# MLP 1's first pair: the second batch by Strassen's scheme, with the orders of VectorE and ScalarE written out

## The chip, the cores and the metric

The kernel runs on one core of one Trainium2 chip. The metric is the device time of one execution in microseconds (us), the median of several runs. The engines are called as in the profile: PE is TensorE (PEld its weight loads), DVE is VectorE, ACT is ScalarE, POOL is GpSimd, SP is SyncE, whose queue issues the DMAs here.

## What the kernel must compute

Clustered attention on 2 batches of 8 heads, whose output `x` (1536 tokens of 512) goes through two MLPs. The change is in the first one and at its seam to the second:

```python
x = np.ascontiguousarray(attn_out.transpose(0, 2, 1, 3)).reshape(B * S, H * D)
h = x @ w_in                            # MLP 1: 1536 x 512 by 512 x 2048
g = h * (1.0 / (1.0 + np.exp(-h)))
x = g @ w_out                           # 2048 x 512
gate = 1.0 / (1.0 + np.exp(-(x @ w_gate)))   # MLP 2, hidden width 1536
out = (gate * (x @ w_val)) @ w_out2
```

## The kernel before

**Precision.** Every fp32 operand is split into a rounded part `hi` and a rest `lo` (fp32r). A product is then three chains of matmuls, hi·hi, hi·lo and lo·hi. ACT makes `hi` by a cast (L65), DVE or POOL makes `lo` by a subtraction (L81 for x and its sums, L1003 for the silu's result, L807 for weights).

**Products.** MLP 1 works in 8 pairs of blocks of 128 hidden units. `x` is stored transposed, as four quarters "11", "12", "21", "22" (half of the model width by half of a batch's tokens); a quarter of one batch is 128 x 768, its halves of a token range 384 wide. `strassen` computes the 2 x 2 block product with 7 products, called x, y, z, w, X, v, W in the order of issue, instead of 8: each has 6 matmuls of 128 x 384 for each batch. Products y, z, w and v take sums of weights (`wi0s`, `wi0t`, ...) and sums of x's quarters (`T1` to `T4`; split into `t1` to `t4`). Their results are put together by additions on DVE (L957), a copy by ACT (L967, of product x) and silu on ACT (L1026). A name such as `h_0y` is product y of the call that begins at batch 0; the trace uses it for both batches when one call does both (128 x 768). The tensors `gha` and `gla` are the hi and lo of silu's result, and `wi2s` is the hi (ACT) and lo (POOL) of the weight sum s for pair 2.

**The first pair** is mixed with the end of the attention. Batch 0 goes through Strassen's scheme there, beside the last attention heads. Batch 1 is finished by the last attention products, and is computed by `direct` (tiles `p`, L1013): the plain 2 x 2 block product, two groups of 24 matmuls. `T1` to `T4` of batch 1 are made later (L94 to L105), since pair 1 is the first to need them. After that come the output products y (L1064) of the first pair, per batch, and from then on each pair's first two h products (`steps(following, n=2)`: x and y), then the output products of the pair before (`mixed`), then the other five.

**Weights** arrive by DMA as 64-bit words (`ri`, `ro`, two buffers) and are converted in integer passes: ACT casts (L764), POOL clamps (L767), DVE makes three passes (L778, L780, L782; for the gate L775 and L782), then ACT and POOL split the result, and POOL makes the sums `si` (L827 to L830).

**Order.** In the first pair and all of MLP 1, `tc.manual_schedule` fixes PE's order to that of the code; the other engines' orders come from the scheduler. Lists such as `behind` and `paced` put an instruction of a conversion behind a given other instruction in that order (`behind` those of DVE, `paced` those of ACT), one entry for one instruction. Every engine executes its own row of instructions strictly in that order.

Of the kernel before, what the change touches and what calls it, by code (L numbers as in the profile page):

```python
# [32 lines left out]
def clustered_attention_then_two_mlps(ctx, tc, qT, kT, v, cen, cenT, w1i, w1o, w2g, w2v, w2o, out):  # L33
# [55 lines left out]
    def right_sums(temporary, name, b, caster, adder, kept):  # L89

        put = partial(right_operand, name, b, caster=caster, subber=adder)
        b11, b21, b12, b22 = quarters(b).values()
        t1 = temporary(f"{name}t1{b}")
        adder.tensor_tensor(t1, b12, b11, op=ALU.subtract)  # L94
        kept[b] = t1
        t2 = temporary(f"{name}t2{b}")
        adder.tensor_tensor(t2, b22, t1, op=ALU.subtract)
        put("t2", t2)
        yield
        t4 = temporary(f"{name}t4{b}")  # L100
        adder.tensor_tensor(t4, t2, b21, op=ALU.subtract)
        put("t4", t4)
        yield
        t3 = temporary(f"{name}t3{b}")
        adder.tensor_tensor(t3, b22, b12, op=ALU.subtract)  # L105
        put("t3", t3)
        yield

    def scheme_operands(temporary, name, b, caster, adder):
# [26 lines left out]
        return make  # L136

    def right_last(name, b, src, caster, subber):
        right_operand(name, b, "t1", src, caster, subber)

    rp = ctx.enter_context(tc.tile_pool(name="rp", bufs=2))
    with ExitStack() as att:
# [861 lines left out]

    def direct(w, name, take, b):

        for m in range(2):
            o = bank(f"{name}_{b}{m}", (ppa, ppb)[m])
            for h in range(2):
                for r in range(2):  # L1010
                    for k in range(KQ):
                        for n, (s, t) in enumerate(((0, 0), (0, 1), (1, 0))):
                            nc.tensor.matmul(  # L1013
                                o[:, h, 0:HS],
                                lhsT=w[f"a{m + 1}{r + 1}"][s][:, k, :],
                                rhs=right[b, f"{r + 1}{h + 1}"][t][:, k, :],
                                start=r == 0 and k == 0 and n == 0,
                                stop=r == 1 and k == KQ - 1 and n == 2,
                            )
            take(o[:, :, 0:HS], m, b)  # L1020
            yield
# [9 lines left out]
    def hidden_directly(i, b):  # L1031
        def take(c, m, b):
            g = temporary(f"g{i}_{m}_{b}")
            nc.scalar.activation(g, c, AF.Silu)
            split(g, m, (slice(0, 2), b), f"a{i}", nc.vector)

        yield from direct(weights("1i", i), f"p{i}", take, b)

# [35 lines left out]
    def gated(i, bs, together=False):  # L1074
# [7 lines left out]
        def value(c, m, h, bs, inside):  # L1082
# [135 lines left out]
    def sums(name, b):
        return right_sums(temporary, name, b, ACT, DVE, kept)

    def last(name, b):
        right_last(name, b, kept.pop(b), ACT, DVE)

# [52 lines left out]

    subs = []

    def rounding(m, h):
        late.pop((m, h))(subs)  # L1280

    def splitting():
        subs.pop(0)()

    def split_now(m, h):
        late.pop((m, h))()
# [135 lines left out]
```

## Time and profile before

| | us |
|---|---|
| median of 3 runs | 768.45 (768.21 to 768.61) |
| the profiled execution: own time / span | 767.51 / 765.7 |
| PE busy / weight loads | 755.2 (99%) / 648.9 (85%) |
| DVE busy | 597.7 (78%) |
| ACT busy | 425.9 (56%) |
| POOL busy | 389.7 (51%) |
| granted clock of PE | full in all 40 slices |

Busy time is the sum over an engine's instructions, and the profiled execution's own time holds 1.8 us outside the span. The shares are means over stages with different limits; the stages that the change touches lie between 230 and 320 us (end of the attention, pairs 0 to 2) and about 445 us (last pair of MLP 1 before MLP 2's gate begins).

### The profile page before, as it was taken

Reading aid. Unit: us, or ns where it says so; the run is one execution under the profiler, and the core shown is the slowest. Engines: PE = TensorE matmul, PEld = TensorE weight load, DVE = VectorE, ACT = ScalarE, POOL = GpSimd, SP = SyncE. Lnnn points to the kernel's source line nnn. Section 1 sums busy time; section 2 is a strip of 40 time slices with the busy share of each in tenths; the row PEclk is TensorE's granted clock in tenths of the full one; section 3 lists DMA queues with packets and bytes.
Section 4 is the critical chain, followed back from the end, with each engine's and each line's share of the span. In section 5 each row is a group of like instructions: output and inputs, shape, how many; then the busy total and the mean of one; then the engine's idle time right before and its main releaser. Section 6 shows DMA issues by size and latency. Waiting matters only on the chain.

```text
span 765.7 us, 11470 instructions
## 1 busy us (share of the span) xinstructions
PE 755.2 (99%) x4289; PEld 648.9 (85%) x4290; DVE 597.7 (78%) x773; ACT 425.9 (56%) x742; POOL 389.7 (51%) x361
## 2 busy tenths in 40 slices
PE   8999999999999999999999999999999999999997
PEld 4766776677767998998989989999999989999896
DVE  7887887788788968798978587986697767859566
ACT  6777776776886762534615545565544525353320
POOL 5235134644655773566647456125776745565430
PEclk9999999999999999999999999999999999999999
DMA  7677457447122122132222120010313112111104
GB/s 209 168 210 192 115 151 195 117 128 193 45 77 72 66 83 83 41 125 83 83 83 73 66 82 1 29 56 27 110 56 108 58 55 97 68 57 56 55 1 166
DMA packets 25488, 71.61 MB, mean 94 GB/s; under 512 B 4484, under 2 KB 4952, under 8 KB 25432
## 3 DMA queue, kind: packets, MB, share of 16 engines
q1 hardware_dynamic: 24888, 70.84, 30.7%
q8 instruction: 34, 0.56, 0.3%
q14 instruction: 22, 0.18, 0.1%
q10 hardware_dynamic: 544, 0.03, 0.0%
HBM read 48.01 MB, written 3.19 MB: 67 GB/s over the span
## 4 chain that ended last, share of the span: by engine, by line
PE 92%; DVE 3%; ACT 2%; DMA 1%; issue 1%; POOL 0%; SPq 0%; ACTq 0%
PE z L1134 13%; PE s L501 8%; PE v L551 7%; PE t L538 5%; PE y L1064 4%; PE h_0w L943 4%; PE h_0x L943 4%; PE v_0x L943 3%; PE g_0w L943 3%; PE g_0x L943 3%; PE v_0w L943 3%; PE y_00None L1064 2%; PE y_21None L1064 2%; PE y_20None L1064 2%; PE y_11None L1064 2%; PE y_10None L1064 2%
## 5 line engine op out<-in xcount | busy, mean ns | idle before, releaser
L514 ACT ACTIVATE e<-s,nm 128x768 f32<-128x768 f32 x96 | 86.5, 901 | 33.8 <-DVE nm L509 32.7
L509 DVE TENSOR_REDUCE nm<-s 128x1 f32<-128x768 f32 x96 | 91.4, 953 | 10.3 <-PE s L501 8.6
L1134 PE MATMUL z<-wu,ghb 128*128 128x512 f32 (+1 forms) x292 | 89.1, 387 | 0.0
L551 PE MATMUL v<-ph,vv 128*64 128x384 f32 x384 | 69.0, 495 | 0.1
L1134 PEld LDWEIGHTS z<-wu,ghb 128*128 128x128 f32 x292 | 54.5, 188 | 10.8
L501 PE MATMUL s<-ka,qa 128*128 128x384 f32 x192 | 57.5, 380 | 2.0 <-ACT e L514 1.5
L538 PE MATMUL t<-ident,e 128*128 128x128 f32 x384 | 58.4, 275 | 0.1
L1134 PE MATMUL z<-wu,glb 128*128 128x512 f32 (+1 forms) x146 | 56.7, 388 | 0.0
L538 PEld LDWEIGHTS t<-ident,e 128*128 128x128 f32 x384 | 44.9, 140 | 11.3 <-issue 9.0
L551 PEld LDWEIGHTS v<-ph,vv 128*64 128x64 f32 x384 | 24.7, 136 | 32.7 <-issue 29.0
L501 PE MATMUL s<-k,q 128*128 128x384 f32 x192 | 49.6, 339 | 0.0
L65 ACT ACTIVATE ph<-t 128x512 f32<-128x512 f32 x68 | 40.6, 598 | 12.6 <-PE t L538 12.0
L1043 DVE TENSOR_TENSOR acc<-z,acc 128x1024 f32<-128x1024 f32 x24 | 29.2, 1221 | 21.6 <-PE z L1134 21.6
L68 DVE COPY ph<-u 128x512 f32<-128x512 f32 x48 | 32.7, 682 | 16.3 <-PE u L528 16.3
L582 POOL TENSOR_TENSOR acc<-xf,rb 128x768 f32<-128x768 f32 x7 | 12.9, 1837 | 59.2 <-DMA rb<-d_rb 56.5
L807 POOL TENSOR_TENSOR wu<-cu,wu 128x512 fp32r<-128x512 f32 x12 | 16.3, 1356 | 52.0 <-ACT wu L65 52.0
L807 POOL TENSOR_TENSOR wo<-co,wo 128x512 fp32r<-128x512 f32 x16 | 24.1, 1510 | 33.5 <-ACT wo L65 33.4
L501 PEld LDWEIGHTS s<-k,q 128*128 128x128 f32 x192 | 34.5, 188 | 0.5 <-DMA k<-rows 0.3
L501 PEld LDWEIGHTS s<-ka,qa 128*128 128x128 f32 x192 | 28.9, 190 | 6.9 <-ACT e L514 5.9
L1064 PE MATMUL y<-gha,wo 128*128 128x384 f32 x128 | 32.8, 334 | 0.0
L1134 PEld LDWEIGHTS z<-wu,glb 128*128 128x128 f32 x146 | 27.4, 188 | 6.0 <-DVE glb L1003 0.5
L563 DVE TENSOR_TENSOR xf<-v,other 64x384 f32<-64x384 f32 x32 | 17.7, 553 | 14.8 <-ACT other L560 14.3
(709 smaller groups left out, 2151.9 us busy)
## 6 DMA issues: line engine op xcount, KB each, us to landing
ri<-in_w1i SPq DMA_DIRECT2D x16, 512.0 KB, 3.2
ro<-in_w1o SPq DMA_DIRECT2D x16, 512.0 KB, 3.1
ka<-kh SPq DMA_DIRECT2D x32, 192.0 KB, 3.6
rg<-in_w2g SPq DMA_DIRECT2D x12, 512.0 KB, 3.6
rv<-in_w2v SPq DMA_DIRECT2D x12, 512.0 KB, 3.1
ru<-in_w2o SPq DMA_DIRECT2D x12, 512.0 KB, 3.2
qq<-in_qT SPq DMA_DIRECT2D x8, 384.0 KB, 3.6
kk<-in_kT SPq DMA_DIRECT2D x8, 384.0 KB, 4.1
```

Source lines behind the costliest of these rows:

```text
L65: return nc.scalar.activation(o, i, AF.Copy)
L68: return nc.vector.tensor_copy(o, i)
L501: nc.tensor.matmul(s[:, g, 0:HS], lhsT=a[:, j, i * P : (i + 1) * P], rhs=c[:, j, g * HS : (g + 1) * HS], start=n == 0, stop=n == 1,)
L509: maxima.append(nc.vector.tensor_reduce(nm, s[:, :, 0:HS], axis=AX.XY, op=ALU.max, negate=True))
L514: x = nc.scalar.activation(e, s[:, :, 0:HS], AF.Exp, bias=nm, scale=1.0, accum_out=tots[p][:, n : n + 1])
L538: nc.tensor.transpose(t[:, kt, :], e[:, kt * P : (kt + 1) * P], ident)
L551: m = nc.tensor.matmul(o[(L, U)[kt % 2]], lhsT=vv[:, j, kt, :], rhs=ring[:, kt, g * G : (g + 1) * G], start=n < 2, stop=n >= NT - 2,)
L807: nc.gpsimd.tensor_tensor(lo, src, hi, op=ALU.subtract)
L943: nc.tensor.matmul(o[:, b, 0:HS], lhsT=w[a][s][:, k, :], rhs=right[b, q][t][:, k, :], start=start and k == 0 and n == 0, stop=k == KQ - 1 ...
L1043: added.append(nc.vector.tensor_tensor(z if to is None else to, o, z, op=ALU.add))
L1064: nc.tensor.matmul(o[:, d, 0:width], lhsT=s[:, d, k, :], rhs=t[:, c], start=k == 0 and m == 0, stop=k == 1 and m == 2,)
L1134: nc.tensor.matmul(o[:, a, c], lhsT=s[:, q * P : (q + 1) * P], rhs=r[:, c], start=k == 0 and m == 0, stop=k == 1 and m == 2, skip_group_ch ...
```

## The change

Batch 1 of the first pair goes through `strassen` too, in the order x, X, y, z, w, v, W, with its products set between those of batch 0. Its operands `T1` to `T4`, `t1` to `t4`, 21 and 22 are made before that, in an order that the code now writes out for DVE and ACT as well, up to the last `lo` of the first pair. Quarter "12" of batch 1 is no longer split by itself (it serves only as `t1`). The DVE passes of pair 1's `ci` weights stand behind the last `lo` of the first pair (`behind.extend(parted * 6)`). The passes of the gate's first weights (`cg`) stand behind a later DVE addition, that of h_7's d of the first batch (`sum_of_w`). The line numbers move: L957 becomes L939, L967 L949, L81 L114, L1003 L985 (L1202 in the first pair), L1026 L990, L1064 L1024, L764 L743, L778/780/782 L757/759/761, L563/637 L540/615.

```diff
-    def direct(w, name, take, b):
-        for m in range(2):
-            o = bank(f"{name}_{b}{m}", (ppa, ppb)[m])
...
-    def hidden(i, bs, order="xyzwXvW"):
+    def hidden(i, bs, order="xyzwXvW", apart=False):
         def take(c, m, h, bs, inside):
             g = c if inside else temporary(f"g{i}_{m}{h}{bs.start}")[:, bs]
             nc.scalar.activation(g, c, AF.Silu)
-            split(g, m, (h, bs), f"a{i}", nc.gpsimd if m and h else nc.vector)
+            parts = partial(split, g, m, (h, bs), f"a{i}", nc.gpsimd if m and h else nc.vector)
+            if apart:
+                late[bs.start, m, h] = parts
+            else:
+                parts()
...
+                if c == place["2g", 0]:
+                    behind.extend(sum_of_w * 4)
...
-    for q in ("11", "12"):
-        right_quarter("x", 1, q, POOL, POOL)
-    for q in ("21", "22"):
-        right_quarter("x", 1, q, ACT, DVE)
-    front = hidden(0, ONE[0], "xwXyzvW")
-    steps(front, n=1)
+    right_quarter("x", 1, "11", POOL, POOL)
+    one = scheme_operands(temporary, "x", 1, ACT, DVE)
+    with tc.issue_after(finished[0].ins):
+        one("T1")
+    zeroth = partial(steps, hidden(0, ONE[0], "xwXyzvW", True))
+    zeroth(n=1)
     look[0] = AHEAD
     weights("1i", 0)
-    steps(front, n=5)
-    following = hidden_directly(0, 1)
-    next(following)
-    run(front)
-    run(following)
+    order = tc.manual_schedule(engines={mybir.EngineType.PE, mybir.EngineType.DVE, mybir.EngineType.Activation})
+    first = partial(steps, hidden(0, ONE[1], "xXyzwvW", True))
+    one("+21")
+    zeroth(n=1)
+    one("+22")
+    zeroth(n=1)
+    one("T2", "T3", "+t2")
+    zeroth(n=1)
+    one("t2", "+t3")
+    rounding(0, 0, 0)
+    zeroth(n=1)
+    first(n=1)
+    one("+t1")
+    splitting(0, 1, 1)
+    one("21", "t3")
+    zeroth(n=1)
+    rounding(0, 1, 0)
+    one("T4", "+t4", "t1")
+    zeroth(n=1)
+    first(n=1)
+    rounding(0, 0, 1)
+    paced.extend(rounded * 2)
+    first(n=1)
+    one("t4", "22")
+    splitting(0, 0, 0)
+    splitting(0, 1, 0)
+    rounding(1, 0, 0)
+    first(n=2)
...
+    order = tc.manual_schedule(engines={mybir.EngineType.PE})
+    order.__enter__()
+    behind.extend(parted * 6)
     weights("1o", 0, 1)
-    rest = sums("x", 1)
-    next(rest)
-    with tc.issue_after(parted[0].ins):
-        run(rest)
-    last("x", 1)
     run(mixed(0, 0))
     run(mixed(0, 1))
     run(hidden(1, ALL))
     for i in range(2, N1):
         following = hidden(i, ALL) if i < N1 - 1 else hidden(i, ONE[0], "xyzXwvW")
         steps(following, n=2 if i < N1 - 1 else 5)
+        if i == N1 - 1:
+            sum_of_w[:] = critical[-1:]
         run(mixed(i - 1, first=int(i == N1 - 1)))
```

How the change moves instructions is shown at three places. The first is DVE from the last attention products (`xf`, and the product into `acc` that completes `x` of batch 1) to the `lo` of the first silu result, `gla_0` from `g_000`. The first output product y needs that `lo` in its second matmul. `x_...` and `xt_...` are `lo` of a quarter or of a sum, `xtt_...` the sums T1 to T4. Before:

```order
L563 TENSOR_TENSOR xf_2780<-v_1_1_2914,other_1_1_2921 64x384
L637 TENSOR_TENSOR acc<-xf_2780,rb_1_2927 128x384
L81 TENSOR_TENSOR x_3047<-acc,x_3047 128x768
L957 TENSOR_TENSOR h_0u_3054<-h_0y,h_0u_3054 128x384
L778 TENSOR_SCALAR ci_0_3208<-ci_0_3208 128x512
L81 TENSOR_TENSOR x_3050<-acc,x_3050 128x768
L957 TENSOR_TENSOR h_0u_3111<-h_0z,h_0u_3054 128x384
L1003 TENSOR_TENSOR gla_0_3100<-g_000_3097,gha_0_3099 128x384
L780 SCALAR_TENSOR_TENSOR ci_0_3208<-ri_0_3206,ci_0_3208 128x512
L778 TENSOR_SCALAR ci_1_3216<-ci_1_3216 128x512
L957 TENSOR_TENSOR h_0d<-h_0w,h_0u_3111 128x384
L782 SCALAR_TENSOR_TENSOR ci_0_3208<-ri_0_3206,ci_0_3208 128x512
```

After, the same place, first half:

```order
L96 TENSOR_TENSOR xtt_3044<-acc 128x768
L540 TENSOR_TENSOR xf_2780<-v_1_1_2914,other_1_1_2921 64x384
L615 TENSOR_TENSOR acc<-xf_2780,rb_1_2927 128x384
L96 TENSOR_TENSOR xtt_3099<-acc,xtt_3044 128x768
L96 TENSOR_TENSOR xtt_3101<-acc 128x768
L939 TENSOR_TENSOR h_0u_3047<-h_0y,h_0u_3047 128x384
L114 TENSOR_TENSOR xt_3103<-xtt_3099,xt_3103 128x768
L939 TENSOR_TENSOR h_0u_3119<-h_0z,h_0u_3047 128x384
L939 TENSOR_TENSOR h_0d<-h_0w,h_0u_3119 128x384
L114 TENSOR_TENSOR x_3080<-acc,x_3080 128x768
```

And directly on, to that `lo`:

```order
L114 TENSOR_TENSOR xt_3114<-xtt_3101,xt_3114 128x768
L939 TENSOR_TENSOR h_0u_3119<-h_0u_3119,h_0v 128x384
L96 TENSOR_TENSOR xtt_3158<-xtt_3099,acc 128x768
L114 TENSOR_TENSOR xt_3140<-xtt_3044,xt_3140 128x768
L939 TENSOR_TENSOR h_0u_3047<-h_0w,h_0u_3047 128x384
L939 TENSOR_TENSOR h_1u_3132<-h_1y,h_1u_3132 128x384
L114 TENSOR_TENSOR xt_3160<-xtt_3158,xt_3160 128x768
L114 TENSOR_TENSOR x_3089<-acc,x_3089 128x768
L1202 TENSOR_TENSOR gla_0_3117<-g_000_3097,gha_0_3116 128x384
```

Ahead of `gla_0` from `g_000` there now stand four sums T and six `lo` of batch 1, each 128 x 768, where there stood two `lo`; the passes of `ci` are gone from between. On PE, the output product y that takes this `lo` stands right behind the first matmul of product v of batch 1 (tile `h_1v`).

The second place is ACT around the rounding of pair 2's weight sums, `wi2s` and `wi2t`. `h_0u_3564` (after: `h_0u_3578`) is the copy of pair 2's product x, the silu on `h_0u_3394` (after: `h_0u_3408`) that of pair 1's last product W; PE issues pair 2's x, then pair 2's y, which takes `wi2s`. Before:

```order
L65 ACTIVATE wi2s<-si_3527 128x512
L764 ACTIVATE co_1_3554<-ro_1_3552 128x512
L65 ACTIVATE gha_0_3471<-g_000_3469 128x768
L65 ACTIVATE wi2t<-si_3527 128x512
L1026 ACTIVATE h_0u_3422<-h_0u_3422 128x768
L65 ACTIVATE gha_1_3453<-h_0u_3422 128x768
L1026 ACTIVATE h_0u_3394<-h_0u_3394 128x768
L967 ACTIVATE h_0u_3564<-h_0x 128x768
L65 ACTIVATE gha_0_3471<-h_0u_3394 128x768
```

After:

```order
L990 ACTIVATE h_0u_3436<-h_0u_3436 128x768
L743 ACTIVATE co_0_3557<-ro_0_3555 128x512
L65 ACTIVATE gha_1_3467<-h_0u_3436 128x768
L990 ACTIVATE h_0u_3408<-h_0u_3408 128x768
L949 ACTIVATE h_0u_3578<-h_0x 128x768
L743 ACTIVATE co_1_3568<-ro_1_3566 128x512
L65 ACTIVATE gha_0_3485<-h_0u_3408 128x768
L65 ACTIVATE wi2s<-si_3541 128x512
L65 ACTIVATE wi2t<-si_3541 128x512
```

The rounding of `wi2s` stood seven rows ahead of the copy of pair 2's x, and stands three rows behind it now. On DVE, the six passes of pair 2's `ci` weights, of which `wi2s` is made, now stand together between pair 1's additions d and v; the `lo` of two silu results and the addition of product W follow.

The third place is DVE at the last pair of MLP 1, with the passes of `cg`, the gate's first weights; the addition that makes `h_0u_4834` (after: `h_0u_4848`) from `h_0y` frees the bank of the output product `y_00None` that opens the next `mixed`. Before:

```order
L775 SCALAR_TENSOR_TENSOR cg_0_5062<-cg_0_5062,rg_0_5060 128x512
L782 SCALAR_TENSOR_TENSOR cg_0_5062<-rg_0_5060,cg_0_5062 128x512
L957 TENSOR_TENSOR h_0d<-h_0w,h_0u_4692 128x768
L957 TENSOR_TENSOR h_0u_4692<-h_0u_4692,h_0v 128x768
L1003 TENSOR_TENSOR gla_0_4742<-g_000_4739,gha_0_4741 128x768
L957 TENSOR_TENSOR h_0u_4580<-h_0w,h_0u_4580 128x768
L775 SCALAR_TENSOR_TENSOR cg_1_5070<-cg_1_5070,rg_1_5068 128x512
L782 SCALAR_TENSOR_TENSOR cg_1_5070<-rg_1_5068,cg_1_5070 128x512
L1003 TENSOR_TENSOR gla_1_4724<-h_0u_4692,gha_1_4723 128x768
L957 TENSOR_TENSOR h_0u_4834<-h_0y,h_0u_4834 128x384
L957 TENSOR_TENSOR h_0u_4850<-h_0z,h_0u_4834 128x384
L1003 TENSOR_TENSOR gla_0_4742<-h_0u_4580,gha_0_4741 128x768
```

After:

```order
L939 TENSOR_TENSOR h_0u_4706<-h_0u_4706,h_0v 128x768
L985 TENSOR_TENSOR gla_0_4756<-g_000_4753,gha_0_4755 128x768
L939 TENSOR_TENSOR h_0u_4594<-h_0w,h_0u_4594 128x768
L985 TENSOR_TENSOR gla_1_4738<-h_0u_4706,gha_1_4737 128x768
L939 TENSOR_TENSOR h_0u_4848<-h_0y,h_0u_4848 128x384
L939 TENSOR_TENSOR h_0u_4864<-h_0z,h_0u_4848 128x384
L985 TENSOR_TENSOR gla_0_4756<-h_0u_4594,gha_0_4755 128x768
L939 TENSOR_TENSOR h_0d<-h_0w,h_0u_4864 128x384
L754 SCALAR_TENSOR_TENSOR cg_0_5076<-cg_0_5076,rg_0_5074 128x512
L754 SCALAR_TENSOR_TENSOR cg_1_5084<-cg_1_5084,rg_1_5082 128x512
L761 SCALAR_TENSOR_TENSOR cg_0_5076<-rg_0_5074,cg_0_5076 128x512
L761 SCALAR_TENSOR_TENSOR cg_1_5084<-rg_1_5082,cg_1_5084 128x512
```

All four passes of `cg` now stand behind the addition `h_0d` of pair 7.

## Rows read from the trace of the kernel before

**Rows 1.** Page part 1, busy time of each engine, and the span.

```profile
span 765.7 us, 11470 instructions
PE 755.2 (99%) x4289; PEld 648.9 (85%) x4290; DVE 597.7 (78%) x773; ACT 425.9 (56%) x742; POOL 389.7 (51%) x361
```

**Rows 2.** Waits of PE, whole span: us in total, times, longest.

```profile
PE y_00None L1064 <- DVE h_0u L957: 0.4, 1, 0.4
```

**Rows 3.** The chain that ended last, from 238 us: start, us, what.

```profile
238.30 1.26 PE h_0w L943 x6
...
244.03 4.16 PE p L1013 x24
...
249.24 4.16 PE p L1013 x24
...
272.25 2.08 PE h_0y L943 x12
...
284.73 2.08 PE h_0x L943 x12
286.81 2.08 PE h_0y L943 x12
```

**Rows 4.** Timeline of PE, 440 to 446 us: start, us, instruction, idle before.

```profile
445.09 0.50 PE L1064 MATMUL y_00None<-gha,wo 128*128 128x512 f32 x1 [0.43 <-DVE h_0u L957]
```

**Rows 5.** Timeline of DVE, 436 to 446 us, same columns.

```profile
442.06 0.92 DVE L775 SCALAR_TENSOR_TENSOR cg<-cg,rg 128x512 int32<-128x512 int32 x1
443.01 0.69 DVE L782 SCALAR_TENSOR_TENSOR cg<-rg,cg 128x512 int32<-128x512 int32 x1
```

**Rows 6.** Timeline of DVE, 238 to 290 us.

```profile
241.23 0.96 DVE L81 TENSOR_TENSOR x<-acc,x 128x768 fp32r<-128x768 f32 x1 [1.22 <-ACT x L65]
242.11 0.55 DVE L957 TENSOR_TENSOR h_0u<-h_0y,h_0u 128x384 f32<-128x384 f32 x1
242.58 0.42 DVE L778 TENSOR_SCALAR ci<-ci 128x512 int32<-128x512 int32 x1
...
247.78 1.18 DVE L782 SCALAR_TENSOR_TENSOR ci<-ri,ci 128x512 int32<-128x512 int32 x1
...
253.58 1.50 DVE L94 TENSOR_TENSOR xt<-acc 128x768 f32<-128x768 f32 x1
...
263.00 0.94 DVE L105 TENSOR_TENSOR xt<-acc 128x768 f32<-128x768 f32 x1
...
273.61 0.69 DVE L780 SCALAR_TENSOR_TENSOR ci<-ri,ci 128x512 int32<-128x512 int32 x1
```

**Rows 7.** Timeline of POOL, 237 to 288 us.

```profile
237.14 2.53 POOL L807 TENSOR_TENSOR wo<-co,wo 128x512 fp32r<-128x512 f32 x2 [2.93 <-ACT wo L65]
...
257.69 2.00 POOL L807 TENSOR_TENSOR wi1s<-si,wi1s 128x512 fp32r<-128x512 f32 x1
...
284.06 1.32 POOL L807 TENSOR_TENSOR wi2s<-si,wi2s 128x512 fp32r<-128x512 f32 x1
```

**Rows 8.** Timeline of ACT, 282 to 290 us.

```profile
282.38 0.62 ACT L65 ACTIVATE wi2s<-si 128x512 fp32r<-128x512 f32 x1
282.89 0.68 ACT L764 ACTIVATE co<-ro 128x512 f32<-128x512 f32 x1
283.47 0.84 ACT L65 ACTIVATE gha<-g 128x768 fp32r<-128x768 f32 x1
284.20 0.62 ACT L65 ACTIVATE wi2t<-si 128x512 fp32r<-128x512 f32 x1
...
287.09 0.85 ACT L1026 ACTIVATE h_0u<-h_0u 128x768 f32<-128x768 f32 x1 [0.66 <-DVE h_0u L957]
287.84 0.79 ACT L967 ACTIVATE h_0u<-h_0x 128x768 f32<-128x768 f32 x1
288.53 0.83 ACT L65 ACTIVATE gha<-h_0u 128x768 fp32r<-128x768 f32 x1
```

**Rows 9.** Page part 6, DMA issues: KB each, us from issue to landing.

```profile
ri<-in_w1i SPq DMA_DIRECT2D x16, 512.0 KB, 3.2
```

More of the change, by code (lines that the diff above doesn't have):

```diff
@@ L59, in clustered_attention_then_two_mlps @@
     maxima = []
-    copied, latest, moved, firsts, added = [], [], [], [], []
+    copied, latest, moved, firsts, added, finished = [], [], [], [], [], []
     home = {0: xp}
@@ L87, in right_quarter @@
         right_operand(name, b, q, quarters(b)[q], caster, subber, "t1" if q == "12" else None)
[L89 to L107, printed above, removed]
     def scheme_operands(temporary, name, b, caster, adder):
@@ L136, in scheme_operands @@
         return make
-    def right_last(name, b, src, caster, subber):
-        right_operand(name, b, "t1", src, caster, subber)
     rp = ctx.enter_context(tc.tile_pool(name="rp", bufs=2))
@@ L636, in finish_last @@
                     )
-            nc.vector.tensor_tensor(
-                acc[:, hp, h, b, :], xf[p][:, h * HS : (h + 1) * HS], rb[:, 0:HS], op=ALU.mult
+            finished.append(
+                nc.vector.tensor_tensor(
+                    acc[:, hp, h, b, :], xf[p][:, h * HS : (h + 1) * HS], rb[:, 0:HS], op=ALU.mult
+                )
             )
@@ L867, in clustered_attention_then_two_mlps @@
     coming, ready = {}, {}
+    sum_of_w = []
     def come(*key, apart=False):
@@ L1003, in split @@
         parted[:] = [subber.tensor_tensor(lo, src, hi, op=ALU.subtract)]
-    def direct(w, name, take, b):
-        for m in range(2):
-            o = bank(f"{name}_{b}{m}", (ppa, ppb)[m])
[L1009 to L1021, printed above, removed]
-    def hidden(i, bs, order="xyzwXvW"):
+    def hidden(i, bs, order="xyzwXvW", apart=False):
         def take(c, m, h, bs, inside):
@@ L1026, in take @@
             nc.scalar.activation(g, c, AF.Silu)
-            split(g, m, (h, bs), f"a{i}", nc.gpsimd if m and h else nc.vector)
-        yield from strassen(weights("1i", i), f"h{i}", take, bs, order)
[L1031 to L1037, printed above, removed]
+            parts = partial(split, g, m, (h, bs), f"a{i}", nc.gpsimd if m and h else nc.vector)
[3 more added lines that the diff above has]
+                parts()
+        yield from strassen(weights("1i", i), f"h{i}", take, bs, order)
     def accumulate(z, o, first, to=None):
@@ L1090, in value @@
             if together:
-                late[m, h] = parts
+                late[bs.start, m, h] = parts
             else:
@@ L1213, in run @@
             pass
-    kept = {}
     ACT, DVE, POOL = nc.scalar, nc.vector, nc.gpsimd
[L1218 to L1222, printed above, removed]
     ONE = [slice(b, b + 1) for b in range(B)]
@@ L1228, in clustered_attention_then_two_mlps, with rounding, splitting @@
     weights("1i", 0)
-    for q in ("11", "12"):
-        right_quarter("x", 1, q, POOL, POOL)
-    for q in ("21", "22"):
-        right_quarter("x", 1, q, ACT, DVE)
-    front = hidden(0, ONE[0], "xwXyzvW")
-    steps(front, n=1)
+    right_quarter("x", 1, "11", POOL, POOL)
[4 more added lines that the diff above has]
+    zeroth(n=1)
     look[0] = AHEAD
     weights("1i", 0)
-    steps(front, n=5)
-    following = hidden_directly(0, 1)
-    next(following)
-    run(front)
-    run(following)
-    weights("1o", 0, 1)
-    rest = sums("x", 1)
-    next(rest)
-    with tc.issue_after(parted[0].ins):
-        run(rest)
-    last("x", 1)
+    order.__exit__(None, None, None)
+    order = tc.manual_schedule(engines={mybir.EngineType.PE, mybir.EngineType.DVE, mybir.EngineType.Activation})
+    order.__enter__()
+    subs = {}
+    def rounding(*key):
+        subs[key] = []
+        late.pop(key)(subs[key])
+    def splitting(*key):
+        if key not in subs:
+            rounding(*key)
+        parted[:] = [subs.pop(key)[0]()]
+    first = partial(steps, hidden(0, ONE[1], "xXyzwvW", True))
[25 more added lines that the diff above has]
+    first(n=2)
+    splitting(0, 0, 1)
+    splitting(1, 1, 1)
+    first(n=1)
+    rounding(1, 1, 0)
+    first(n=1)
+    rounding(1, 0, 1)
+    splitting(1, 0, 0)
+    splitting(1, 1, 0)
+    splitting(1, 0, 1)
+    order.__exit__(None, None, None)
+    order = tc.manual_schedule(engines={mybir.EngineType.PE})
+    order.__enter__()
+    behind.extend(parted * 6)
+    weights("1o", 0, 1)
     run(mixed(0, 0))
@@ L1275, in clustered_attention_then_two_mlps @@
     passes("2o", 0, 0)
[L1277 to L1286, printed above, removed]
     go = partial(steps, gated(0, ONE[0], True))
@@ L1291, in clustered_attention_then_two_mlps @@
     parted_weights("2o", 0, 0)
-    rounding(0, 0)
+    rounding(0, 0, 0)
     go(n=2)
-    splitting()
+    splitting(0, 0, 0)
     zero("22")
@@ L1303, in clustered_attention_then_two_mlps @@
     go(n=4)
-    rounding(1, 0)
+    rounding(0, 1, 0)
     go(n=1)
-    splitting()
-    split_now(1, 1)
+    splitting(0, 1, 0)
+    splitting(0, 1, 1)
     go(n=1)
-    rounding(0, 1)
+    rounding(0, 0, 1)
     one("21")
-    splitting()
+    splitting(0, 0, 1)
     outs = out_of(0)
@@ L1326, in clustered_attention_then_two_mlps @@
     one("+22")
-    rounding(0, 0)
+    rounding(1, 0, 0)
     go(n=2)
-    splitting()
+    splitting(1, 0, 0)
     one("t4")
@@ L1334, in clustered_attention_then_two_mlps @@
     go(n=4)
-    rounding(1, 0)
+    rounding(1, 1, 0)
     go(n=1)
-    splitting()
-    split_now(1, 1)
+    splitting(1, 1, 0)
+    splitting(1, 1, 1)
     go(n=1)
-    split_now(0, 1)
+    splitting(1, 0, 1)
     critical.append(parted[0])
```

## The prediction

> **What bounds the kernel now.** I read the page's busy times first: PE is busy 755.2 of 765.7 us, every other engine 78% or less [rows 1]. So time can come only from fewer or shorter matmuls, or from PE's waits. The list of PE's waits comes second: the only one behind the attention is 0.4 us at an output product y [rows 2]. Third the chain of waits: from 238.30 us on it is PE alone, product after product without a gap; five of its rows stand in [rows 3]. Two readings follow. A matmul that is taken out there gives its whole time back. And any other engine that comes late by a microsecond there costs a whole microsecond, for PE has no idle time to swallow it. So I price the removed matmuls, then go through what PE waits for in the new orders, and ask of each: when is it ready, when is it due?
>
> **Term A, the matmuls.** `direct` issues two groups of 24, each 4.16 us, 0.1733 us a matmul [rows 3]. Strassen's scheme has 42 in place of 48: −6 × 0.1733 = **−1.04 us**. The products themselves are of the same shape (128x384).
>
> **Term B, the gate's passes.** `y_00None` at 445.09 us has an idle time of 0.43 ahead, released by DVE's `h_0u` [rows 4]. Ahead of that addition DVE ran two passes of `cg` and a `gla`, from 442.06 on [rows 5]. The change puts the passes behind the later `h_0d`. DVE comes to the `gla` and the addition 1.6 us (0.92 + 0.69) earlier then, so the 0.43 goes; PE's matmul before it also came late to its end, so up to 0.85 may come back. I take **−0.6** (−0.43 to −0.85). The `cg` passes come a few microseconds later for the gate's weights, whose products begin only after the output products of pair 6, twelve matmuls six times over; that hides it.
>
> **Term C, the first output product y.** Its second matmul takes `gla_0`. From T1 to that `lo`, DVE has 19 rows in the new order: ten of 128x768, nine of 128x384 or less. Rows that follow each other at once give the price: a wide one 0.88 (241.23 to 242.11), a narrow one 0.47 (242.11 to 242.58) [rows 6]. That is 8.8 + 4.2 = 13.0 us. In the changed program T1 waits for the end of the last attention product v, 238.30 [rows 3], so the `lo` ends at 251.4 at best. PE, from 238.30, has twelve products of 6 and one y matmul ahead: 73 × 0.1733 = 12.65, due 251.0. So the stretch, which had slack, is bound by DVE: floor 0.4 us. To it come waits inside it: t2's `lo` needs ACT's rounding of T2, T1's successors follow on each other's ends; I put 0.8 on them, from the tail (a wide one lasts 0.94 to 0.96, 0.08 more than its pitch [rows 6]) and one exposed rounding. And POOL works beside it: wo until 239.67 [rows 7], then clamps and a `gla`. The same subtraction of two quarters took 1.50 beside POOL and 0.94 without [rows 6], so three wide rows hit cost 1.7. Sum 0.4 + 0.8 + 1.7 = **+2.9** (0.4 to 3.3).
>
> The price of that contention can be weighed. The row of 1.50 does not say whether the subtraction ran slowly or stood still 0.56 and then ran 0.94. The Trainium skill ("SBUF — State Buffer", section "Who interferes with whom") says the second: DVE's second port pair is GpSimd's, held as an exclusive lock, and the one that issues later blocks until the first is done. By it T1, issued at 238.3, just ahead of POOL's second wo, would take 0.94 and wo would pay; the sum would be 0.6 less, some 775.3. The trace bears both readings, and I keep the row's.
>
> **Term D, pair 2's product y.** Here the order of ACT changes most. With A and C, PE is 2.9 − 1.04 = 1.9 late when it comes to pair 1: pair 2's x starts at 284.73 + 1.86 = 286.6, its y is due at 288.7 [rows 3]. In the order before, `wi2s` was rounded at 283.00, 3.8 us ahead of y's start at 286.81, and POOL's half was done at 285.38 [rows 3, 7, 8]. Now ACT has the copy of pair 2's x first, and the copy cannot start before x ends, at 288.7, the very moment at which y is due. Whatever else happens, y waits. The price, from starts of rows that follow each other on ACT: copy 0.69 (287.84 to 288.53), the cast `co` 0.58 (282.89 to 283.47), `gha` 0.73 (283.47 to 284.20), the rounding itself 0.62 [rows 8]: 2.6 us. Then POOL's `lo`, 1.32 [rows 7] and some 0.1 to start, is needed by y's fifth matmul, 4 × 0.1733 = 0.7 later (for both batches the lo comes after the four matmuls that take `hi`): another 0.7. **Floor of D: 3.4.**
>
> More comes where ACT gets to the copy late. Ahead of it stands the silu of product W, which waits for DVE's addition W. DVE's row there: d (ends near 281.3), six passes of `ci`, v, two `gla`, with W between. Three passes, by rows of 0.42, 0.69 and 0.69 to 1.18 that overlap by 0.08 each, are 1.6 to 2.05 [rows 6]; two sets 3.1 to 4.1, so to 284.4 to 285.4. The addition v 0.88, one `gla` 0.88 to 1.9 (one beside POOL, like the 1.50), the addition W 0.88: 287.0 to 289.1, and 0.5 more if the passes wait for their DMA and clamp. Silu 0.75 (287.09 to 287.84 [rows 8]) then puts the copy at 287.8 to 290.4, against 288.7. Beyond the floor that is up to 1.7, and POOL's half may come later, up to 1.6, as POOL has clamps and a `gla` of its own there. D is 3.4 to 6.7. I take **+5.5**, above the middle, since every DVE row ahead of W has to be at its shortest for the floor.
>
> **Term E, smaller waits.** `wi1s`, for pair 1's y, hangs on the `ci` passes that were moved behind the last `lo` of the first pair. Before, they ended at 248.96, and POOL's half of `wi1s` 10.7 later, at 259.69 [rows 6, 7]. Now C's `lo` at 253.9 is followed by eleven narrow rows (5.2) and the six passes (3.7): 262.8, and with the same 10.7, 273.5. Pair 1's y is due at 272.25 + 1.86 = 274.1 [rows 3], its fifth matmul 0.7 later. So it just fits, or costs up to 0.9. `y_11` of pair 1 needs a bank that DVE's addition of `y1_00` frees, which now stands behind the passes of pair 3's `ci_0`: that load is issued after the last `co` pass, near 295; then DMA 3.2 [rows 9], ACT's cast 0.58 and, as my estimate, 4 for the clamp, three passes and the addition: 302.8, against a due time of some 304 (y_11 is the fourth of the output products behind pair 2's y, and they go three at a time through the banks): 0 to 1.5. I take **+0.7** for both (0 to 2.3).
>
> **What is moved and costs nothing:** the four sums T of batch 1 and their roundings were made beside the first pair's y; taken from there they free DVE by some 6 us where the `ci` and `co` passes now go. POOL loses the split of quarter "12", time it did not lack. Later pairs: their weight chain starts about 3 us later while PE is 7 us later, so I see no further stall.
>
> **Sum:** −1.04 − 0.6 + 2.9 + 5.5 + 0.7 = +7.5. The rows are from an execution of 767.51 us, where it gives 775.0; the median of the runs shown is 768.45, 0.9 above, so **775.9**.
>
> **Rivals.**
> *The savings alone (other side).* If ACT rounds `wi2s` ahead of the copy of pair 2's x in time, that is by 285.8 (286.81 − 1.04) with POOL's half 0.7 later, and DVE's stretch ends by 251.0, only A and B are left: 768.45 − 1.64 = 766.8. For it: DVE is busy 78% and ACT 56% [rows 1], there is time enough to round in, and 19 rows at their shortest are only 0.4 late. Against it: the copy of x comes first in ACT's order, and an engine does not overtake in its row. Chance 0.04.
> *The floor.* C costs 0.4 to 1.3, D its 3.4, E nothing: +2.2 to +3.1, 770.6 to 771.5. For it: the additions that take a product's bank kept 0.55 in the one row shown [rows 6], so not every row need pay. Chance 0.08.
> *No change.* D or C much shorter than worked out, stalls of 0.1 to 3.2 in all, within 0.2% (1.54 us, about the least that a measurement of this kernel can tell from no change). It needs pair 2's weights to be rounded early, and only C to fail. Chance 0.04.
> *The delay goes on.* Pairs 3 to 7 get their weights as late as pair 2, and pay again, one or two microseconds each: 780 to 786. For it: each pair's conversion begins when the buffers `ri` of the one before are free. Against it: the order before shows no wait in pairs 3 to 6 with the same chain, and a PE that is 7 us late leaves more room. Chance 0.06.
> *The forecast,* both waits, 771.5 to 779.3: 0.78.
>
> **How the numbers follow.** The sum is the likeliest case's. The ends of the terms are −1.04 − 0.85 + 0.4 + 3.4 + 0 = +1.9 and −1.04 − 0.43 + 3.3 + 6.7 + 2.3 = +10.8; on the median, 770.4 and 779.3. That is my range: it holds the forecast and the floor and leaves out the other three rivals, 0.14. Faster by over 0.2% 0.04, within 0.2% 0.04, slower 0.92.
>
> **What the profile after would show.** For A: 42 h_1 matmuls, no tile `p`. For B: no wait at y_00None near the seam. For C: a wait of the first y for `gla`, near 251 to 254, with DVE in it without idle time from 238.3. For D: a wait of pair 2's h_0y for ACT's `wi2s`, and a second for POOL's, with ACT's copy of x directly after x ends and then the cast, `gha` and rounding. For E: waits at pair 1's y and at y_11. The prediction is wrong if the wait at pair 2's y is under 3 us, if DVE's stretch keeps slack, or if PE waits in pairs 3 to 7 as well.

## The result and the profile after

| | before | after |
|---|---|---|
| median, us | 768.33 (768.17 to 768.61, 4 runs) | 777.49 (776.95 to 778.09, 4 runs) |
| ratio to before | | 1.0119 (95%: 1.0101 to 1.0137) |
| profiled execution: own time / span | 767.51 / 765.7 | 776.95 / 775.2 |

The change makes the kernel 9.2 us slower; 775.9 was forecast, in a range of 770.4 to 779.3. The page of the changed kernel, part 1, the answer to [rows 1]:

```profile
span 775.2 us, 11476 instructions
PE 757.7 (98%) x4283; PEld 649.1 (84%) x4284; DVE 602.3 (78%) x779; ACT 427.8 (55%) x747; POOL 383.0 (49%) x360
```

PE has six matmuls less, and is busy 2.5 us longer. Matmuls that were slower must stand behind that; the granted clock shows them below. The waits of PE from 238 us on (us in total, times, longest), the answer to [rows 2]:

```profile
PE h_0y L925 <- ACT wi2s L65: 5.5, 1, 5.5
PE h_1w L925 <- DVE h_0u L939: 0.9, 1, 0.9
PE y L1024 <- DVE gla L1202: 0.5, 1, 0.5
PE h_0w L925 <- DVE h_0d L939: 0.3, 1, 0.3
PE y_11None L1024 <- DVE acc L1003: 0.2, 1, 0.2
```

Of the waits that the forecast named, those of y for `gla`, of pair 2's h_0y for ACT and of y_11 are there, and the gate's is gone. The second one of pair 2's h_0y, for POOL's `wi2s`, and the one at pair 1's y are not there, and those at h_0w and h_1w were not named. The timeline of PE at those places (start, us, instruction, idle before and releaser) says where time was lost, if each start is held against the same instruction before:

```profile
238.32 1.34 PE L925 MATMUL h_0w<-xt,wi0s 128*128 128x384 f32 x6
...
253.78 0.45 PE L1024 MATMUL y<-gla,wo 128*128 128x384 f32 x1 [0.49 <-DVE gla L1202]
...
271.76 2.24 PE L925 MATMUL h_0x<-x,wi1a 128*128 128x384 f32 x12
...
286.32 2.34 PE L925 MATMUL h_0x<-x,wi2a 128*128 128x384 f32 x12
294.11 4.34 PE L925 MATMUL h_0y<-xt,wi2s 128*128 128x384 f32 x12 [5.45 <-ACT wi2s L65]
298.28 0.39 PE L1024 MATMUL y_00None<-gha,wo 128*128 128x512 f32 x1
...
315.14 2.27 PE L925 MATMUL h_0z<-xt,wi2t 128*128 128x384 f32 x12
...
454.55 0.39 PE L1024 MATMUL y_00None<-gha,wo 128*128 128x512 f32 x1
```

Before, the first mark lay at 238.23, and the five behind it (pair 1's x, pair 2's x, y_00None of pair 1, pair 2's z, y_00None at the seam) at 270.01, 284.57, 288.73, 305.09 and 445.09 [rows 4]. In the timeline before:

```profile
238.23 1.33 PE L943 MATMUL h_0w<-xt,wi0s 128*128 128x384 f32 x6
...
270.01 2.24 PE L943 MATMUL h_0x<-x,wi1a 128*128 128x384 f32 x12
...
284.57 2.24 PE L943 MATMUL h_0x<-x,wi2a 128*128 128x384 f32 x12
286.65 2.24 PE L943 MATMUL h_0y<-xt,wi2s 128*128 128x384 f32 x12
288.73 0.39 PE L1064 MATMUL y_00None<-gha,wo 128*128 128x512 f32 x1
...
305.09 2.27 PE L943 MATMUL h_0z<-xt,wi2t 128*128 128x384 f32 x12
```

The lag is 0.09 at 238, then 1.75, 1.75, 9.55, 10.05 and 9.46. So: A and C together +1.66 (with A = −1.04, C is 2.70), nothing in pair 1, D 7.80, then 0.50 at y_11, and −0.59 at the seam; sum with the 0.09: 9.46, against 9.44 between the two own times.

D is larger than its wait of 5.45. The rest is the speed behind it: the windows of PE (us, busy time, granted clock, DMA share, GB/s), same stretch:

```profile
288.00:290.00 2.00, 0.65 (x4) 1.00 0.71 211
290.00:292.00 2.00, 0.00 (x0) 0.81 0.13 51
292.00:294.00 2.00, 0.00 (x0) 0.50 0.00 0
294.00:296.00 2.00, 1.89 (x5) 0.50 0.02 4
...
298.00:300.00 2.00, 2.00 (x11) 0.98 0.29 51
```

While PE stood still the granted clock fell from 1.00 to 0.50, which is 1.2 of 2.4 GHz, and came back at 298. y's twelve matmuls (294.11 to 298.28) took 4.17 us, where the same twelve took 2.08 before: 2.1 us more, not in any list of waits. The 0.26 that is left of the 7.80 lies at the end of x: from its start to the idle time 2.34 us pass, and from x to y before 2.08.

What y waited for, on ACT and on POOL and DVE (timelines, same columns; the answers to [rows 8, 7, 6]):

```profile
290.71 0.84 ACT L990 ACTIVATE h_0u<-h_0u 128x768 f32<-128x768 f32 x1 [0.19 <-DVE h_0u L939]
291.46 0.79 ACT L949 ACTIVATE h_0u<-h_0x 128x768 f32<-128x768 f32 x1
292.15 0.65 ACT L743 ACTIVATE co<-ro 128x512 f32<-128x512 f32 x1
292.70 0.83 ACT L65 ACTIVATE gha<-h_0u 128x768 fp32r<-128x768 f32 x1
293.44 0.62 ACT L65 ACTIVATE wi2s<-si 128x512 fp32r<-128x512 f32 x1
```

```profile
237.30 3.25 POOL L786 TENSOR_TENSOR wo<-co,wo 128x512 fp32r<-128x512 f32 x2 [2.99 <-ACT wo L65]
...
290.36 0.72 POOL L807 TENSOR_TENSOR si<-si,ci 128x256 f32<-128x256 f32 x1
```

```profile
238.44 0.96 DVE L96 TENSOR_TENSOR xtt<-acc 128x768 f32<-128x768 f32 x1 [1.60 <-PE v L528]
...
248.39 1.77 DVE L114 TENSOR_TENSOR xt<-xtt,xt 128x768 fp32r<-128x768 f32 x1
...
252.76 0.96 DVE L1202 TENSOR_TENSOR gla<-g,gha 128x384 fp32r<-128x384 f32 x1
...
259.47 0.56 DVE L939 TENSOR_TENSOR h_1u<-h_1w,h_1u 128x384 f32<-128x384 f32 x1 [2.81 <-PE h_1w L925]
...
283.44 2.35 DVE L759 SCALAR_TENSOR_TENSOR ci<-ri,ci 128x512 int32<-128x512 int32 x1
285.82 1.67 DVE L761 SCALAR_TENSOR_TENSOR ci<-ri,ci 128x512 int32<-128x512 int32 x1
```

ACT's row is what the order said: silu, copy, cast, gha, rounding, one directly behind the other, started by DVE's addition W. But look at POOL: the sum `si` of which `wi2s` is the rounding was itself finished only at 291.08, since the last pass of pair 2's `ci` ended on DVE at 287.49. Two chains end at this wait, 2.4 us apart, and the forecast priced only the longer one. DVE, that had little idle time up to 256.7, then stood idle for 2.81 us, with pair 1's passes held back behind a later row. These points made the experiments.

### The profile page after: what moved, and what is told of

Read it like the earlier page. It is cut to its first block, busy times and chain, and to the rows that moved or that the text cites. A ratio compares the mean times of both kernels' runs of the same rounds, so it can differ in the third digit from the quotient of the medians.

```text
span 775.2 us, 11476 instructions
## 1 busy us (share of the span) xinstructions
PE 757.7 (98%) x4283; PEld 649.1 (84%) x4284; DVE 602.3 (78%) x779; ACT 427.8 (55%) x747; POOL 383.0 (49%) x360
## 4 chain that ended last, share of the span: by engine, by line
PE 63%; DVE 4%; issue 1%; ACT 1%; POOL 0%
PE z L1094 13%; PE y L1024 4%; PE h_0w L925 3%; PE g_0w L925 3%; PE v_0x L925 3%; PE g_0x L925 3%; PE v_0w L925 3%; PE h_0x L925 3%; PE y_11None L1024 2%; PE y_21None L1024 2%; PE y_20None L1024 2%; PE y_00None L1024 2%; PE h_0z L925 2%; PE y_10None L1024 2%; PE y_01None L1024 2%; PE g_0z L925 1%
## 5 line engine op out<-in xcount | busy, mean ns | idle before, releaser
L1003 DVE TENSOR_TENSOR acc<-z,acc 128x1024 f32<-128x1024 f32 x24 | 29.2, 1222 | 21.2 <-PE z L1094 21.2
L1024 PE MATMUL y<-gha,wo 128*128 128x384 f32 x128 | 32.9, 334 | 0.0
L540 DVE TENSOR_TENSOR xf<-v,other 64x384 f32<-64x384 f32 x32 | 17.7, 553 | 12.7 <-ACT other L537 12.2
```

Source lines behind the costliest of these rows:

```text
L1003: added.append(nc.vector.tensor_tensor(z if to is None else to, o, z, op=ALU.add))
L1024: nc.tensor.matmul(o[:, d, 0:width], lhsT=s[:, d, k, :], rhs=t[:, c], start=k == 0 and m == 0, stop=k == 1 and m == 2,)
```

## The experiments

One theory is the prediction's: ACT's order (rounding behind the copy of x) is the floor of term D. The other: the weights of pair 2 are late by themselves, because the six passes of pair 1's weights were moved behind the first pair. (The text of e2 numbers its two theories for itself.) A third question is what the clock costs. Ratios are to the kernel before, measured beside it on the same chip, with 95% intervals.

**e1, the gate's passes alone, in the kernel before.**

```diff
+                if c == place["2g", 0]:
+                    behind.extend(sum_of_w * 4)
...
+        if i == N1 - 1:
+            sum_of_w[:] = critical[-1:]
```

> The kernel before with one part of the change: the four passes of the gate's first weights stand behind the addition h_0d of pair 7. Theory (term B): the wait of y_00None for DVE at 445 us goes, 0.43 to 0.85 us, so 767.5 to 767.9 against 768.33, and no other wait behind the attention comes up. Rival: the passes are then late for the gate's first product, a new wait near 470 us of a microsecond or more, so 769 or above.

Measured 766.75 against 767.78, ratio 0.9987 (0.9978 to 0.9996): 1.0 us less, a little more than expected, but the interval holds what was expected. PE's list of waits has no row behind 238 us any more, and in the trace the seam comes 0.62 earlier, counted from the product at 238 us. That is term B, and this kernel is faster than both.

**e2, the moved passes alone, in the kernel before.**

```diff
     run(following)
+    behind.extend(parted * 6)
     weights("1o", 0, 1)
```

> The kernel before with one part of the change: the six passes of pair 1's ci weights stand behind the last lo of the first pair; batch 1 of the first pair stays the plain block product. Theory 1 (the late weights): moving these passes from about 245 to about 260 us makes every later conversion late, so that pair 2's y waits for wi2s 3 to 6 us without any Strassen product of batch 1, and pays again at a lower granted clock behind the wait: 772 to 777. Theory 2 (the delay comes with Strassen's operands on DVE): without those operands DVE has the time, the conversion catches up, and the wait at pair 2's y is under 1 us: 768 to 769.5.

Measured 775.63, ratio 1.0102 (1.0089 to 1.0116): +7.85 us, without one product changed. Waits of PE from 238 us on:

```profile
PE h_0y L943 <- ACT wi2s L65: 4.8, 1, 4.8
...
PE h_0y L943 <- POOL wi2s L807: 0.4, 1, 0.4
PE h_0y L943 <- POOL wi1s L807: 0.3, 1, 0.3
```

This is term D, clock included, reproduced by one line: from pair 2's x to y_00None it loses 7.4 us, where the changed kernel lost 7.8, and another 0.5 ahead of that, with the wait at pair 1's y. The passes of pair 1 end at 264.4 in it (248.96 before [rows 6]), the load of pair 2's `ri` is issued at 271.95 instead of 264.61, and all that follows is late. Strassen's operands are not needed for it. The same line also turns ACT's order round. Here too the rounding of `wi2s` now stands behind the copy of pair 2's x, with the sum ready at 290.64:

```profile
290.71 0.79 ACT L967 ACTIVATE h_0u<-h_0x 128x768 f32<-128x768 f32 x1
291.40 0.62 ACT L65 ACTIVATE wi2s<-si 128x512 fp32r<-128x512 f32 x1
```

**e3, `wi2s` rounded as early as its input allows, in the changed kernel.** The silu of W and the copy of x stand behind it on ACT. `roundings` holds the rounding of each weight sum by its name; the first added line writes pair 2's conversions earlier in the code, so that the name exists.

```diff
+    weights("1o", 1, 0)
     run(hidden(1, ALL))
...
+            with tc.issue_after(roundings["i2s"].ins) if (i, m, h) == (1, 0, 1) else nullcontext():
+                nc.scalar.activation(g, c, AF.Silu)
...
+                with tc.issue_after(roundings["i2s"].ins) if name == "h2_0" else nullcontext():
+                    nc.scalar.activation(column("u2"), q, AF.Copy)
```

> The changed kernel, with ACT's rounding of wi2s ahead of the silu of pair 1's W and of the copy of pair 2's x (both are put behind it), nothing else moved. Theory of the prediction (ACT's order is the floor of term D): with the order undone the wait of pair 2's y for ACT falls from 5.45 us to under 1, and the time by 4 us or more, to 773.5 or less. Rival (late weights): the rounding cannot begin before POOL's sum si, whose row in the changed kernel ends at 291.1 us; the wait for ACT falls to 2.5 to 3.2 only, POOL's lo takes over another 1.5 to 2, and the silu and the copy that now stand behind make y_11's wait longer: 775.5 to 778.

Measured 777.04, ratio 1.0123 (1.0109 to 1.0137): nothing gained. Waits of PE at that place:

```profile
PE h_0y L927 <- ACT wi2s L65: 3.4, 1, 3.4
PE h_0y L927 <- POOL wi2s L788: 2.0, 1, 2.0
```

The sum is ready at 291.54 and the rounding starts at 291.76, so the wait for ACT fell by 2.0, as far as the late sum let it (an ACT cast just ahead of it waited for its own late DMA), and POOL's `lo` took it back. Undoing the order that I had called the floor is worth nothing while the sums are late.

**e4, pair 1's passes put into DVE's idle 2.81 us, in the changed kernel.**

```diff
+    early = critical[-1:]
     first(n=1)
     rounding(1, 0, 1)
...
-    behind.extend(parted * 6)
+    behind.extend(early * 6)
```

> The changed kernel, with the six passes of pair 1's ci weights behind the addition of product v of batch 1 instead of behind the last lo of the first pair, so in the 2.81 us that DVE stood idle at 256.7. ACT's order keeps the rounding of wi2s behind the copy of pair 2's x. Theory of the prediction: the floor of term D stays, a wait of 2.6 to 3 us at pair 2's y for ACT, and POOL's lo after it; the part above the floor goes: 773 to 774.5. Late weights: every later conversion comes 3 to 5 us earlier, and the wait at pair 2's y falls from 5.45 by that much, to 0.5 to 2.5, and with a wait that short the granted clock stays up: 771 to 773.5.

Measured 775.17, ratio 1.0098 (1.0084 to 1.0111). Waits at that place, and the windows of PE behind them:

```profile
PE h_0y L925 <- ACT wi2s L65: 3.3, 1, 3.3
...
PE h_0y L925 <- POOL wi2s L786: 0.6, 1, 0.6
```

```profile
290.00:292.00 2.00, 0.03 (x1) 1.00 0.00 0
...
294.00:296.00 2.00, 2.00 (x8) 0.50 0.03 8
...
298.00:300.00 2.00, 2.00 (x7) 0.61 0.91 330
```

Here the sum is ready at 288.8, and ACT's order is what holds the rounding until 291.3: the floor of the prediction, alone, 3.33 where 2.6 to 3 was expected. The wait is 2.1 us shorter than in the changed kernel, but y_01None of pair 1 starts only 0.46 earlier (300.57 for 301.03): the clock falls again, only after the wait, and its 0.50 now lies on a working PE instead of an idle one. With y_11's wait gone too, pair 2's z comes 1.0 earlier, and the ratio says some 1.6 us in all, though its interval meets that of the changed kernel (1.0101 to 1.0137). Both expectations missed the total, 775.17 against 773 to 774.5 and 771 to 773.5, for want of the clock; the second missed the wait as well.

**e5, the wait filled with 24 matmuls that nothing reads.**

```diff
+            for n in range(idle):
+                nc.tensor.matmul(o[:, n % 2, 0:HS], lhsT=w["a11"][0][:, 0, :], rhs=right[n % 2, "11"][0][:, 0, :], start=True, stop=True)
```

> The changed kernel with 24 more matmuls (128x384, a product that nothing reads, overwritten by y's own first matmul) on PE between pair 2's x and y, where PE stood idle for 5.45 us. Theory (the idle costs a second time): in the changed kernel y's twelve matmuls behind the wait ran at a granted clock of 0.50 and took 4.2 us instead of 2.08; with 24 x 0.1733 = 4.2 us of work in the wait the clock stays near 1.00, y's matmuls take 0.173 each, and what is left is POOL's lo of wi2s, which then comes about 1.2 us late: 0.6 to 1.6 us less than the changed kernel although it computes more, 775.9 to 776.9 against its 777.5. Rival (the slow matmuls wait for something else, POOL's lo above all): no gain, within 0.3 us of the changed kernel, or slower.

Measured 776.56, ratio 1.0112 (1.0097 to 1.0127): not to be told from the changed kernel's 1.0119. Waits of 1.30 (ACT) and 0.65 (POOL) were left, and behind them the clock fell all the same:

```profile
298.00:300.00 2.00, 2.00 (x7) 0.50 0.11 27
```

So this run did not test the theory; e10 does.

**e6, both chains undone:** e3 and e4 together, and POOL's `lo` of pair 1's d behind its `lo` of `wi2s`.

```diff
+                with tc.issue_after(roundings["i2s", 0].ins) if (i, m, h) == (1, 1, 1) else nullcontext():
+                    parts()
```

> The changed kernel with both undone at once: the six passes of pair 1's weights 5 us earlier (as in e4), and the rounding of wi2s ahead of the silu of W and of the copy of x on ACT (as in e3), and POOL's half of wi2s ahead of the lo of pair 1's silu result d on POOL. Theory now (two chains end at the same wait, the late sums and ACT's order, and either alone holds it): the wait at pair 2's y falls to 0 to 1.2 us in all, the clock stays up, and terms A, B, C are left: -1.04 - 0.6 + 2.7 + 0.6 = +1.7 on before, 769 to 770.5. Rival (the weights of pair 2 are late whatever the order, since POOL and DVE slow each other): 2.5 us or more of wait remain, and the clock falls again: 772.5 or above.

Measured 769.86 against 767.95, ratio 1.0027 (1.0016 to 1.0038). Of D's waits one is left, and the granted clock is 1.00 throughout:

```profile
PE h_0y L927 <- POOL wi2s L788: 0.9, 1, 0.9
```

e3 gave nothing and e4 some 1.6 us (ratio 1.0098 against 1.0119); together, and with POOL's row, which was not tried by itself, they give 7.

**e7, pair 1's passes not held back at all:** the two lines `paced.extend(rounded * 2)` and `behind.extend(parted * 6)` are taken out of the changed kernel.

> The changed kernel without the two entries that put pair 1's weights behind the first pair (ACT's casts behind a rounding, DVE's passes behind the last lo): the six passes, and the passes of the next output weights, then stand among the operands of batch 1 on DVE. Theory: DVE has no room in that stretch, so term C grows by what is put in, six passes of 0.34 to 0.60 and their waits, 3.2 to 6 us, as waits at h_1z, h_1w, h_1v and y; in exchange pair 2's y waits for nothing and the clock stays up there: 773 to 776. Rival (there is room, the delay was needless): C stays under 4 us and the time falls to 771.5 or less.

Measured 774.31, ratio 1.0082 (1.0065 to 1.0099). Waits of PE from 238 us on, and the windows of PE behind them:

```profile
PE h_1w L925 <- DVE h_0u L939: 2.4, 1, 2.4
PE h_0w L925 <- DVE h_0d L939: 1.7, 1, 1.7
```

```profile
256.00:258.00 2.00, 1.86 (x7) 0.50 0.63 242
```

D is gone: ACT rounds `wi2s` at 289.91, 5 us ahead of the copy of pair 2's x (294.95), as in the order before. C has taken its place: pair 1's x begins 7.6 us later than before, counted from the same v product, with the clock at 0.50 for some of it. In this stretch DVE has no room for the passes.

**e8, one lo moved out of DVE's full stretch,** in the changed kernel.

```diff
-    one("t4", "22")
+    one("t4")
     splitting(0, 0, 0)
     splitting(0, 1, 0)
     rounding(1, 0, 0)
     first(n=2)
+    one("22")
```

> The changed kernel with one row of DVE moved: the lo of quarter 22 of batch 1, which only product W reads, stands behind three lo of silu results instead of ahead of them. Theory (term C: DVE's row is what the first y waits for): gla_0 comes 0.88 us earlier, y's wait of 0.49 and what follows it go, 0.5 to 1.1 us less at pair 1's x; but the wait at pair 2's y grows by as much, for the late weights do not come earlier: within 0.5 us of the changed kernel, 777.0 to 777.9. Rival (PE's delay at y is what sets everything behind it): 776.3 to 776.9.

Measured 775.77, ratio 1.0103 (1.0088 to 1.0118), against 1.0119. y's wait for `gla` is gone, pair 1's x comes 1.1 us earlier, and the wait at pair 2's y did not grow (5.16 for ACT and 0.28 for POOL, where it was 5.45). My expectation was wrong here. The traces show what the rival says: the passes of pair 1 hang behind the first pair's last `lo`, and pair 2's behind those, so they came earlier with PE. The time lies below the ranges of both, though, and the two ratios' intervals meet.

**e9, e6 and e8 together.**

> e6 with the row of e8 too: passes of pair 1's weights 5 us earlier, wi2s first on ACT and POOL, and the lo of quarter 22 behind three lo of silu results. Theory (terms add when no wait is left behind them to take a gain back): term C falls by the 1.1 us that e8 had at pair 1's x, and as pair 2's wait is under 1.2 us, the gain stays: 0.6 to 1.3 us less than e6, ratio to before 1.0010 to 1.0020, so the batch by Strassen's scheme comes out level with the plain one. Rival: PE comes 1.1 us earlier to pair 2's y and waits that much longer for wi2s: ratio 1.0024 to 1.0030, as e6.

Measured 769.39 against 767.91, ratio 1.0018 (1.0009 to 1.0027). The ratio is what the theory said, but its interval reaches into the rival's range and overlaps that of e6 (1.0016 to 1.0038), so the times do not decide. Waits of PE from 238 us on:

```profile
PE h_0y L927 <- POOL wi2s L788: 1.1, 1, 1.1
...
PE h_0z L927 <- DVE acc L1009: 0.7, 1, 0.7
```

The traces speak for the rival: counted from the product at 238 us, pair 1's x comes 1.1 us earlier than in e6, and pair 2's z no earlier at all, with a longer wait at pair 2's y and a new one at z. The kernel comes to 0.18% of the one before, but not ahead of it. And part of that is the gate's: e1, the plain batch with the gate's passes moved, stands at 0.9987, so against it the batch by Strassen's scheme is still some 0.3% behind.

**e10, the wait filled with 36 matmuls** (the edit of e5, another count).

> The changed kernel with 36 matmuls that nothing reads, 6.2 us, between pair 2's x and y, so that they cover the wait for ACT's and nearly that for POOL's half of wi2s (in e5 24 of them left waits of 1.30 and 0.65 us, and the granted clock fell behind these). Theory: with no wait over 0.5 us left the granted clock stays at 1.00 from 284 to 304 us; y starts 0.8 us later than in the changed kernel but takes 2.08 us instead of 4.2: 1.0 to 1.6 us less than the changed kernel, ratio to before 1.0098 to 1.0106. Rival (the clock falls here whatever PE does): half the speed for some microseconds behind y, ratio 1.0119 or above.

Measured 775.36, ratio 1.0096 (1.0083 to 1.0110), 1.0119 (1.0101 to 1.0137) without the 36; the intervals still meet, so the gain is read from the traces. A wait of 0.17 was left at y, and the clock stayed up:

```profile
294.00:296.00 2.00, 1.83 (x11) 1.00 0.02 4
```

Pair 2's x starts 0.05 later than in the changed kernel, y_00None 0.9 earlier, and z 1.4 earlier, since y_11 does not wait either. More work on PE cost less than the wait.

## Why the prediction was right, and where not

**A, B.** As forecast: 42 matmuls of `h_1` and no tile `p`; the seam gives back 0.59 in the trace (0.6 forecast), and alone (e1) about 1.0 us, with an interval of 0.3 to 1.7.

**C.** 2.70 against 2.9, from waits at h_0w, h_1w and y, of which I had named the last. The list has 1.7 us of them; the other 1.0 lies in slower starts of matmuls around them and was not taken apart. The `lo` that y takes ended at 253.72, 253.9 was worked out, but the parts differ. T1 took 0.96, not 1.50, and POOL's two wo took 3.25 instead of 2.53 [rows 7]. This is what the Trainium skill says ("SBUF — State Buffer", section "Who interferes with whom"): the first to issue keeps its speed, and the other blocks. I kept the row's price for T1, and it was the page's that came out. What made up for it were DVE's wait for the rounding of T2 (0.48) and two rows that issued behind a POOL one (the `lo` of T1 1.77, behind POOL's `gla` of 247.57; `gla` 0.96, behind its clamp of 252.63).

**D.** The place and the chain on ACT were right. That the wait came out as taken, 5.45 idle for 5.5, is in part luck: in the 5.5 stood something for POOL's `lo` (0.7 to 2.3 worked out), and that did not show, as the matmuls ahead of it ran at half speed. ACT's part had been worked out as 2.6 to 4.3, and was 5.45.

Three steps failed. First, a size: the six passes of pair 2's `ci` were to take DVE 3.1 to 4.1 us. They took 6.3, from 281.15 to 287.49, with rows of 2.35 and 1.67 beside POOL where 1.18 was the longest reckoned with. So addition W came late, and with it the copy, at 291.46 instead of 287.8 to 290.4.

Second, the price stopped at the wait: 2.1 us came on top, since PE's granted clock halved during the idle. So D was 7.80 where the top of my range was 6.7.

Third, the step "whatever else happens, y waits", that ACT's order is the floor, is only half of it. Shown by e3, e4 and e6: ACT's order and the late sums each hold the wait, and removing one leaves the other. Shown by e2: what is behind the lateness is the line that puts six passes behind the first pair, which costs 7.85 us by itself in the kernel before, and turns ACT's order round as well. The two chains have one origin. I had put those passes into term E, as a risk of 0.9 for pair 1, and found them harmless there, which they were; I did not follow them one pair further, through the load, the casts and the clamps, to the wait that I had already found.

**E.** 0.50 where 0.7 was taken: y_11 waited for DVE's `acc` as described, pair 1's y for nothing. Later pairs showed no wait, as argued.

**The total.** 775.9 against 777.5: C and E were put 0.4 too high and D 2.3 too low, 1.9 us in the trace and 1.6 between the medians. The rival of the savings alone was never near. Even with both chains undone the change stays behind: in e6 because C, 2.70, costs more than A and B give, and in e9, where C is down to 1.56, because of the waits at pair 2's y and z. A slip without weight: the forecast speaks of five rows in [rows 3], and there are six.

Open: whether a better order of DVE's rows in the first pair could bring C under 1.04; e9 still shows 0.9 at h_1w and 0.3 at h_0w.

## What to carry to other kernels

When a piece of work is put off on an engine with spare time, follow its product to every consumer down the chain of buffers, not only to the next one: here the next pair was served in time and the pair after it was not. Where a wait has an explanation, ask when its other inputs are ready before calling that explanation the floor; two chains that end 2.4 us apart hide each other, and experiments that undo one of them show little (nothing in e3, some 1.6 of 7 us in e4). And price a stall on PE as more than its length where the profile shows the clock falling in it or behind it.

## What the hardware showed that I had not expected

PE's granted clock reacts to one wait in mid-kernel, in it or just behind it. Behind idle stretches of 5.45, 5.16 (e8), 4.76 (e2), 3.41 and 1.97 (e3), 3.33 (e4), 2.41 (e7) and the 1.30 and 0.65 of e5 it was 0.50 for some microseconds. With 0.92 (e6), 1.08 (e9) and 1.66 (e7) it stayed at 1.00. Length alone does not sort these: the 1.30 and 0.65 of e5 stand 1.0 us apart, and the 1.66 of e7 alone. A shorter wait is not a smaller loss by the same amount: in the changed kernel about half of the slow time fell on an idle PE, in e4 nearly all of it on work, so that little of the 2.1 us was left two products on. And 36 matmuls whose result nothing reads made the kernel 1.4 us faster at pair 2's z, 0.9 of it at the first product behind y.
